# The first microseconds of a fused attention and gMLP block: order and split of the first loads, and who makes the first hT

## The chip, the cores and the metric

One core of one Trainium2 chip. The metric is the device time of one execution in microseconds (us), the median of several runs. The profile's span is 1.7 to 1.9 us shorter than the device time of the same execution. "Tile 1" is the second 128 rows of x, and "scores" are the matmuls of Q with K.

## The reference, cut to what matters

```python
mod = (_silu(c) @ w_mod).reshape(c.shape[0], 6, 1, -1)     # c: (1, 512), w_mod: (512, 3072)
sa, ca, ga, sb, cb, gb = (mod[:, i] for i in range(6))
h = _layernorm(x, axis=-1) * (1 + ca) + sa                 # x: (1, 2048, 512)
x = x + ga * _A_ref(h, A_k_cache, A_v_cache, A_wq, A_wo)   # q = h @ wq, 32 heads; 8 K and V heads; softmax; @ wo
h = _layernorm(x, axis=-1) * (1 + cb) + sb
x = x + gb * _B_ref(h, B_w_in, B_w_sp, B_b_sp, B_w_out)    # gMLP
```

All tensors are bf16. Before the first score can be computed the kernel needs: the modulation columns sa and ca (the first 1024 columns of w_mod), x tile 0 normalised, transposed and modulated (hT), the query weights of the first group, and K transposed.

## The kernel before

The prologue is one hand-ordered list of instructions. `warm(n)` issues n matmuls of zeros that nothing reads. `bank("misc")` and `bank("o_ps")` are tiles of one bank in PSUM, the memory into which TensorE (PE in the profiles) writes, `bank2()` one of two banks (s_ps); each name has two buffers. Line numbers in profiles of before: L868 is `mod_part`, L900 the transposes of xn, L883 those of K, L921 the first query product, L929 its two copies, L980 the scores, L846 the tile-1 transposes.

```python
nc.scalar.dma_start(out=c_bf[:], in_=c_dram)
nc.sync.dma_start(out=x_sb[:, 0, :], in_=x_dram[:, 0, :])
for kt in range(NDT):                                       # four row parts, 256 KB each
    nc.sync.dma_start(out=wmod_a[:, kt, :], in_=wmod_dram[:, kt, 0 : 2 * D])
load_k_nat(0)                                               # K, first 512 rows
load_wq(0, nc.sync)                                         # query weights, 512 KB
load_k_nat(1)
nc.sync.dma_start(out=x_sb[:, 1:CT, :], in_=x_dram[:, 1:CT, :])      # x tiles 1 to 3
# ... (K rows 1024 and up by DMA transpose, V, more x)
xns0 = ln1_norm(0, 1, ln1_stats(0, 1))
warm(10)
for kt in range(NDT - 1):
    mod_part(kt, mc_ps)                                     # 8 one-column matmuls
    warm(2)
x_ps = []
for half in range(2):                                       # dt 0, 1 in misc; dt 2, 3 in o_ps
    x_ps.append(bank(("misc", "o_ps")[half])[:].bitcast(BF16))
    # ... two transposes of xn each
mod_part(NDT - 1, mc_ps)
mod_copy(0, mc_ps)
for k in range(2):
    ln1_mod(hTs[0][:, k, 0:P], x_ps[0][:, k * P : (k + 1) * P], k)          # DVE: dt 0, 1
    nc.scalar.activation(out=hTs[0][:, 2 + k, 0:P], in_=x_ps[1][...], ...)  # ACT: dt 2, 3
k_turn((0, 1, 2, 3), (nc.vector.tensor_copy, nc.scalar.copy))               # K, through o_ps
q_ps = bank2()
for n, dt in enumerate((0, 2, 1, 3)):
    # ... four query matmuls, one for each head
for hf, copy in enumerate((nc.vector.tensor_copy, nc.scalar.copy)):
    copy(out=qTs[0][:, 2 * hf : 2 * hf + 2, 0:P], in_=...)  # both halves out of q_ps
warm(1)
# ... units of 8 slots; slot i: score pair i, exp; in unit 0 also tile 1 to 3 of hT and Q
```

## Time and profile before

| | device time, us | note |
|---|---|---|
| first runs | 1323.93 median of 3 | 1323.85 to 1324.84 |
| the profiled run | 1325.52 | span 1323.7; slower than each of the three |
| first rounds with the changed kernel | 1324.12 median of 6 | 1323.85 to 1325.55; the three first runs are among them |
| later rounds | 1324.24, 1324.15, 1324.05 medians of 9 | 1323.75 to 1324.95 |

The prediction below shows the lines on which it rests: the busy time of PE and the chain of waits of the first 16 us.

### The profile page before, as it was taken

What the parts mean: (1) busy time and instruction counts of PE and PEld (TensorE: products, weight loads), DVE (VectorE), ACT (ScalarE), POOL (GpSimd) and SP (SyncE); (2) the same over time, 40 slices, a digit from 0 to 9 for tenths busy, and PEclk for the clock granted to TensorE, in tenths of its full rate; (3) what the DMA queues carried; (4) which work ended last, traced back from release to release, by engine and by line L of the source; (5) the groups of instructions that cost most, each with busy time, mean ns of one, the idle gap of its engine ahead of it and who ended that gap; (6) DMA issues with size and microseconds to landing.
All of it is one profiled execution on the core that took longest, in us unless ns stands there. A gap on an engine that the chain in (4) does not pass through costs nothing.

```text
span 1323.7 us, 27668 instructions
## 1 busy us (share of the span) xinstructions
PE 1303.0 (98%) x12127; PEld 859.5 (65%) x12332; DVE 472.6 (36%) x1166; ACT 1077.6 (81%) x1061; POOL 48.9 (4%) x92
## 2 busy tenths in 40 slices
PE   8999999999999999999999999999999999999998
PEld 5666666666666666666666666666666666644445
DVE  5632222222222222222222222222222566794444
ACT  6898999999999999999999999999999999650000
POOL 1200000000000000000000000000000000020000
PEclk9999999999999999999999999999999999999999
DMA  7451022102111112111110221121101111143300
GB/s 175 114 135 30 17 49 37 36 15 53 21 33 33 33 37 37 29 37 37 33 33 17 53 37 29 21 53 17 33 17 21 25 30 33 33 114 80 70 21 26
DMA packets 148208, 58.12 MB, mean 44 GB/s; under 512 B 138384, under 2 KB 143760, under 8 KB 148080
## 3 DMA queue, kind: packets, MB, share of 16 engines
q1 hardware_dynamic: 141424, 37.78, 15.0%
q0 software_dynamic: 4208, 16.39, 4.1%
q10 hardware_dynamic: 2448, 2.10, 0.5%
q8 instruction: 98, 1.61, 0.5%
q14 instruction: 30, 0.25, 0.1%
HBM read 21.37 MB, written 2.10 MB: 18 GB/s over the span
## 4 chain that ended last, share of the span: by engine, by line
PE 98%; issue 1%; DMA 0%; DVE 0%; SPq 0%; ACT 0%; ACTq 0%
PE s_ps L980 36%; PE o_ps L1002 35%; PE misc L947 7%; PE misc L1347 7%; PE misc L1034 6%; PE s_ps L1193 2%; PE s_ps L1232 2%; PE o_ps L1368 1%; PE s_ps L1368 0%; DMA wmod_a<-in_w_mod_dram 0%; PE misc L1104 0%; PE s_ps L921 0%; DVE tmp L1380 0%; DVE yout L1381 0%; PE misc L1355 0%
## 5 line engine op out<-in xcount | busy, mean ns | idle before, releaser
L987 ACT ACTIVATE pT<-s_ps 128x1024 bf16<-128x1024 f32 x1024 | 1044.3, 1025 | 83.2 <-PE s_ps L980 9.2
L1002 PEld LDWEIGHTS <-pT 128*128 128x128 bf16 x8192 | 548.5, 98 | 241.2
L1002 PE MATMUL o_ps<-v,pT 128*128 128x129 bf16 x8192 | 631.4, 220 | 0.0
L980 PE MATMUL s_ps<-qT,kT 128*128 128x512 bf16 x2048 | 609.2, 379 | 10.2 <-ACT qT L929 0.5
L1013 DVE RECIPROCAL rall<-o_ps 128x2 f32<-128x2 f32 x256 | 43.7, 171 | 744.7 <-PE o_ps L1002 744.5
L980 PEld LDWEIGHTS <-kT 128*128 128x128 bf16 x2048 | 199.4, 98 | 119.2 <-issue 1.4
L947 PE MATMUL misc<-hT,wq_g 128*128 128x512 bf16 (+2 forms) x466 | 166.6, 370 | 0.1
L1034 PE MATMUL misc<-wo_g,oT 128*128 128x512 bf16 x386 | 146.3, 379 | 0.0
L1014 DVE TENSOR_TENSOR onorm<-o_ps,rall 128x256 bf16<-128x256 f32 x256 | 108.6, 424 | 9.0 <-DVE rall L1013 0.3
L1347 PE MATMUL misc<-wsp,z 128*128 128x512 bf16 (+2 forms) x555 | 100.5, 336 | 0.6 <-issue 0.3
L958 DVE CAST qT<-misc 128x512 bf16<-128x512 f32 x127 | 86.3, 680 | 2.4 <-PE misc L947 2.3
L1347 PEld LDWEIGHTS <-z 128*128 128x128 bf16 x560 | 50.6, 98 | 48.5
L1047 DVE TENSOR_TENSOR xacc<-misc,xacc 128x512 f32<-128x512 f32 x112 | 76.1, 679 | 0.0
L947 PEld LDWEIGHTS <-wq_g 128*128 128x128 bf16 x528 | 50.6, 98 | 1.1 <-issue 0.2
L1034 PEld LDWEIGHTS <-oT 128*128 128x128 bf16 x512 | 50.1, 98 | 0.8
L1362 DVE TENSOR_TENSOR gb<-misc,bsp_bc 128x512 bf16<-128x512 f32 (+1 forms) x28 | 18.4, 658 | 59.2 <-PE misc L1347 59.2
L1193 PE MATMUL s_ps<-win_sb,hT 128*128 128x448 bf16 x128 | 27.0, 352 | 0.1
L1203 ACT ACTIVATE z<-s_ps 128x896 bf16<-128x896 f32 x16 | 14.7, 917 | 14.9 <-PE s_ps L1193 14.9
L1232 PE MATMUL s_ps<-hT,win_sb 128*128 128x512 bf16 x109 | 24.3, 379 | 0.2
L1240 ACT ACTIVATE z1T<-s_ps 128x1024 bf16<-128x1024 f32 x14 | 14.3, 1024 | 10.1 <-PE s_ps L1232 9.1
L691 DVE BATCH_NORM_STATS2 bnst<-x_sb 128x6 f32<-128x512 bf16 x32 | 21.9, 683 | 0.5
L715 POOL DMA_DIRECT2D wq_g<-in_A_wq_dram x7 | 5.3, 752 | 420.9 <-PE misc L947 420.9
(86 smaller groups left out, 283.0 us busy)
## 6 DMA issues: line engine op xcount, KB each, us to landing
wq_g<-in_A_wq_dram POOLq DMA_DIRECT2D x7, 512.0 KB, 3.9
v<-in_A_v_cache_dram POOLq DMA_DIRECT2D x7, 512.0 KB, 6.9
wo_g<-in_A_wo_dram POOLq DMA_DIRECT2D x7, 512.0 KB, 4.7
oT<-onorm SPq DMA_TRANSPOSE x128, 2.4
wsp<-in_w_mod_dram POOLq DMA_DIRECT2D x1, 2048.0 KB, 10.3
out_dram<-yout ACTq DMA_DIRECT2D x16, 128.0 KB, 1.7
win_sb<-in_B_w_in_dram POOLq DMA_DIRECT2D x1, 1792.0 KB, 7.9
x_sb<-in_A_x_dram SPq DMA_DIRECT2D x3, 512.0 KB, 5.6
```

Of the source, the lines that this page charges most:

```text
L947: nc.tensor.matmul(ps[0][:, o0 : o0 + n], lhsT=wqs[g][:, dt, hh * DH : (hh + 1) * DH], rhs=hTs[ch][:, dt, c0 : c0 + n], start=(dt == 0), s ...
L958: nc.vector.tensor_copy(out=dst, in_=src)
L980: nc.tensor.matmul(s_ps[:, h * 512 : (h + 1) * 512].rearrange("p (r q) -> p r q", r=REP), lhsT=groups[g]["kT"][:, kt * P : (kt + 1) * P], ...
L987: nc.scalar.activation(out=pTs[u][:, 2 * i : 2 * i + 2, :], in_=s_ps[:].rearrange("p (k q) -> p k q", k=2), func=ACT.Exp, scale=inv_sqrt_dh,)
L1002: nc.tensor.matmul(o_ps[:, hh % 2, 0 : DH + 1], lhsT=pTs[u][:, kt, hh * P : (hh + 1) * P], rhs=groups[g]["v1"][:, kt, 0 : DH + 1], start=( ...
L1013: nc.vector.reciprocal(out=rall[:, c0 : c0 + 2], in_=o_ps[:, :, DH])
L1014: nc.vector.tensor_tensor(out=onorms[u][:, hh - 1 : hh + 1, :], in0=o_ps[:, :, 0:DH], in1=rall[:, c0 : c0 + 2].unsqueeze(2).to_broadcast([ ...
L1034: nc.tensor.matmul(X_ps[:], lhsT=oTs[u][:, hh, :], rhs=groups[g]["wo"][:, hh, :], start=(hh == 0), stop=(hh == REP - 1),)
L1047: nc.vector.tensor_tensor(out=xaccs[j][:], in0=X_ps[:], in1=xaccs[j][:], op=ALU.add)
L1193: nc.tensor.matmul(ps[0][:, hf * 512 : hf * 512 + FC], lhsT=h2Ts[j // CT][:, dt, (j % CT) * P : (j % CT + 1) * P], rhs=win_sb[:, dt, FH + ...
L1232: nc.tensor.matmul(ps[0][:, k * 512 : (k + 1) * 512], lhsT=win_sb[:, dt, f * P : (f + 1) * P], rhs=h2Ts[2 * ch2 + k][:, dt, :], start=(dt ...
L1347: nc.tensor.matmul(g_ps[:, :n], lhsT=z2[:, st, f * P : (f + 1) * P], rhs=wsp[t][:, st, c0 : c0 + n], start=(st == 0), stop=(st == NT - 1 a ...
```

## The change

Its intent: have the modulation columns, the query weights and K land in the order in which the first scores need them, and let the first query matmuls start as soon as one quarter of hT is there.

```diff
-    nc.sync.dma_start(out=x_sb[:, 0, :], in_=x_dram[:, 0, :])
-    for kt in range(NDT):
-        nc.sync.dma_start(out=wmod_a[:, kt, :], in_=wmod_dram[:, kt, 0 : 2 * D])
+    nc.scalar.dma_start(out=x_sb[:, 0, :], in_=x_dram[:, 0, :])
+    for i in range(2):
+        part = slice(i * D, (i + 1) * D)
+        nc.sync.dma_start(out=wmod_a[:, :, part], in_=wmod_dram[:, :, part])
-    load_k_nat(0)
-    load_wq(0, nc.sync)
+    wqs[0] = early.tile([P, NDT, REP * DH], BF16, name="wq_g")
+    for dts in (slice(0, 2), slice(2, 4)):
+        nc.sync.dma_start(out=wqs[0][:, dts, :], in_=wq_dram[:, dts, 0 : REP * DH])
+    load_k_nat(0)
     load_k_nat(1)
# ... mod_part sums a column part, all kt of a column in a row; mod_columns goes (cut)
     warm(10)
-    for kt in range(NDT - 1):
-        mod_part(kt, mc_ps)
-        warm(2)
+    mod_part(0, wmod_a, 0, mc_ps)
+    warm(6)
+    x_ps = [bank("misc")[:].bitcast(BF16), bank2()[:, 0:512].bitcast(BF16)]   # dt % 2 picks one
# ... four transposes of xn
-    mod_part(NDT - 1, mc_ps)
+    mod_part(1, wmod_a, D, mc_ps)
     mod_copy(0, mc_ps)
+    warm(2)
# hT: DVE makes dt 0 and 2, ACT 1 and 3 (before: DVE 0 and 1, ACT 2 and 3)
-    k_turn((0, 1, 2, 3), (nc.vector.tensor_copy, nc.scalar.copy))
-    q_ps = bank2()
-    for n, dt in enumerate((0, 2, 1, 3)):
+    q_ps = [bank("misc"), bank2()]
+    for dt in range(NDT):
+        if dt == 2:
+            k_turn((0, 1, 2, 3), (nc.vector.tensor_copy, nc.scalar.copy))
# ... the query matmuls and the two copies, from q_ps[0] and q_ps[1]
-    warm(1)
+    warm(2)
```

Line numbers in profiles of the changed kernel: L848 modulation, L807 and L899 hT on DVE and ACT, L912 first query product, L870 K transposes, L920 copies of Q, L971 scores, L825 tile-1 transposes, L779 warm-ups.

More of the change, by code (lines that the diff above doesn't have):

```diff
@@ L782, in warm @@
             )
-    def mod_columns(first, wmod, i0):
-        mc_ps = bank("misc")
-        for i in range(2):
-            for dt in range(NDT):
-                col = i * NDT + dt
-                w0 = (first + i - i0) * D + dt * P
-                for kt in range(NDT):
-                    nc.tensor.matmul(
-                        mc_ps[:, col : col + 1],
-                        lhsT=wmod[:, kt, w0 : w0 + P],
-                        rhs=sc_bf[:, kt : kt + 1],
-                        start=(kt == 0),
-                        stop=(kt == NDT - 1),
-                    )
-        mod_copy(first, mc_ps)
-    def mod_copy(first, mc_ps):
-        c0 = first * NDT
-        nc.vector.tensor_copy(out=modc[:, c0 : c0 + NDT], in_=mc_ps[:, 0:NDT])
-        nc.vector.tensor_scalar_add(
-            out=modc[:, c0 + NDT : c0 + 2 * NDT], in0=mc_ps[:, NDT : 2 * NDT], scalar1=1.0
-        )
     def ln1_stats(j0, n):
@@ L863, in ln1_dma_mod, with mod_part, mod_copy @@
             ln1_mod(hTs[ch][:, dt, :], hTs[ch][:, dt, :], dt)
-    def mod_part(kt, mc_ps):
-        for col in range(2 * NDT):
-            nc.tensor.matmul(
-                mc_ps[:, col : col + 1],
-                lhsT=wmod_a[:, kt, col * P : (col + 1) * P],
-                rhs=sc_bf[:, kt : kt + 1],
-                start=(kt == 0 and col == 0),
-                stop=(kt == NDT - 1 and col == 2 * NDT - 1),
-            )
+    def mod_part(i, wmod, w0, mc_ps):
+        for dt in range(NDT):
+            for kt in range(NDT):
+                nc.tensor.matmul(
+                    mc_ps[:, i * NDT + dt : i * NDT + dt + 1],
+                    lhsT=wmod[:, kt, w0 + dt * P : w0 + (dt + 1) * P],
+                    rhs=sc_bf[:, kt : kt + 1],
+                    start=(kt == 0),
+                    stop=(kt == NDT - 1),
+                )
+    def mod_copy(first, mc_ps):
+        c0 = first * NDT
+        nc.vector.tensor_copy(out=modc[:, c0 : c0 + NDT], in_=mc_ps[:, 0:NDT])
+        nc.vector.tensor_scalar_add(
+            out=modc[:, c0 + NDT : c0 + 2 * NDT], in0=mc_ps[:, NDT : 2 * NDT], scalar1=1.0
+        )
     def k_turn(kts, copies):
@@ L891 @@
     warm(10)
-    for kt in range(NDT - 1):
-        mod_part(kt, mc_ps)
-        warm(2)
-    x_ps = []
-    for half in range(2):
-        x_ps.append(bank(("misc", "o_ps")[half])[:].bitcast(BF16))
-        for k in range(2):
-            dt = 2 * half + k
-            nc.tensor.transpose(
-                x_ps[half][:, k * P : (k + 1) * P], xns0[0][:, dt * P : (dt + 1) * P], ident[:]
-            )
-    mod_part(NDT - 1, mc_ps)
+    mod_part(0, wmod_a, 0, mc_ps)
+    warm(6)
+    x_ps = [bank("misc")[:].bitcast(BF16), bank2()[:, 0:512].bitcast(BF16)]
@@ L904 @@
+    for dt in range(NDT):
+        nc.tensor.transpose(
+            x_ps[dt % 2][:, dt // 2 * P : (dt // 2 + 1) * P],
+            xns0[0][:, dt * P : (dt + 1) * P],
+            ident[:],
+        )
+    mod_part(1, wmod_a, D, mc_ps)
     mod_copy(0, mc_ps)
+    warm(2)
     hT_of(0)
     for k in range(2):
-        ln1_mod(hTs[0][:, k, 0:P], x_ps[0][:, k * P : (k + 1) * P], k)
-        nc.scalar.activation(
-            out=hTs[0][:, 2 + k, 0:P],
-            in_=x_ps[1][:, k * P : (k + 1) * P],
-            func=ACT.Identity,
-            scale=modc[:, NDT + 2 + k : NDT + 3 + k],
-            bias=modc[:, 2 + k : 3 + k],
-        )
@@ L915 @@
-    k_turn((0, 1, 2, 3), (nc.vector.tensor_copy, nc.scalar.copy))
+        for dt in (2 * k, 2 * k + 1):
+            dst, src = hTs[0][:, dt, 0:P], x_ps[dt % 2][:, k * P : (k + 1) * P]
+            if dt % 2 == 0:
+                ln1_mod(dst, src, dt)
+            else:
+                nc.scalar.activation(
+                    out=dst,
+                    in_=src,
+                    func=ACT.Identity,
+                    scale=modc[:, NDT + dt : NDT + dt + 1],
+                    bias=modc[:, dt : dt + 1],
+                )
@@ L916 @@
     qTs = {0: early.tile([P, REP, 512], BF16, name="qT")}
-    q_ps = bank2()
-    for n, dt in enumerate((0, 2, 1, 3)):
+    q_ps = [bank("misc"), bank2()]
+    for dt in range(NDT):
+        if dt == 2:
+            k_turn((0, 1, 2, 3), (nc.vector.tensor_copy, nc.scalar.copy))
         for hh in range(REP):
-            c0 = hh // 2 * 512 + hh % 2 * P
             nc.tensor.matmul(
-                q_ps[:, c0 : c0 + P],
+                q_ps[hh // 2][:, hh % 2 * P : (hh % 2 + 1) * P],
                 lhsT=wqs[0][:, dt, hh * DH : (hh + 1) * DH],
@@ L924 @@
                 rhs=hTs[0][:, dt, 0:P],
-                start=(n == 0 and hh % 2 == 0),
-                stop=(n == NDT - 1 and hh % 2 == 1),
+                start=(dt == 0 and hh % 2 == 0),
+                stop=(dt == NDT - 1 and hh % 2 == 1),
             )
@@ L930 @@
             out=qTs[0][:, 2 * hf : 2 * hf + 2, 0:P],
-            in_=q_ps[:, hf * 512 : hf * 512 + 2 * P].rearrange("p (h q) -> p h q", h=2),
+            in_=q_ps[hf][:, 0 : 2 * P].rearrange("p (h q) -> p h q", h=2),
         )
-    warm(1)
+    warm(2)
     def qproj(b, heads, c0, n):
@@ L1099, in mod_lhs, with mod_cols_b @@
         return lhs
+    def mod_cols_b():
+        mc_ps = bank("misc")
+        for i in range(2):
+            mod_part(i, wmod_b, (1 + i) * D, mc_ps)
+        mod_copy(3, mc_ps)
     def mod_row(row_out, i, lhs):
@@ L1155 @@
     at(8, 1, lambda: rest_w.update(lhs=mod_lhs()))
-    at(9, 4, lambda: mod_columns(3, wmod_b, 2))
+    at(9, 4, mod_cols_b)
     at(10, 4, lambda: mod_row(ga_rows, 2, rest_w["lhs"]))
```

## The prediction

> **What bounds the kernel now.** I read the page first, part 1 and part 4. TensorE is busy for 1303.0 of 1323.7 us and the chain that ended last is 98% PE. The parts of it that weigh are the score, value and projection matmuls of the steady state, none of which the change touches.
>
> ```profile
> PE 1303.0 (98%) x12127; PEld 859.5 (65%) x12332; DVE 472.6 (36%) x1166; ACT 1077.6 (81%) x1061; POOL 48.9 (4%) x92
> ...
> PE 98%; issue 1%; DMA 0%; DVE 0%; SPq 0%; ACT 0%; ACTq 0%
> ```
>
> The reader is to see how little is left: 1323.7 - 1303.0 = 20.7 us without a matmul, everywhere in the kernel. The edit is all in the prologue, before the first score matmul (L980), so I read the chain of waits in order of time next, for the first 24 us. Columns: start, duration, what.
>
> ```profile
> 2.14 5.42 DMA wmod_a<-in_w_mod_dram
> 7.60 0.35 PE misc L868 x8
> ...
> 8.85 0.16 DVE modc L803
> 9.01 0.08 DVE modc L804
> 9.18 0.82 ACT hT L908 x2
> 10.04 0.34 PE o_ps L883 x2
> 10.37 1.72 PE s_ps L921 x16
> 12.12 0.44 DVE qT L929
> 12.58 0.38 ACT qT L929
> 13.00 0.83 PE s_ps L980 x2
> 13.83 0.24 PE o_ps L883 x4
> 14.09 0.42 DVE kT L886
> ...
> 15.69 0.40 PE misc L846 x4
> ```
>
> This is one serial string. The modulation weight lands, its columns are summed (L868), copied (L803, L804), applied to hT by ACT (L908); two K transposes wait for ACT because they use the o_ps bank that ACT was reading; then 16 query matmuls; then DVE and, only after it, ACT copy qT; at 13.00 the scores start. From about 24 us on, the same view has PE pieces end to end. So a microsecond taken off this string comes off the end, and nothing bigger than this string can be won. The stretches view (busy time per engine, then granted clock, DMA share, GB/s) shows one more thing:
>
> ```profile
> 9.50:10.00 0.50, 0.00 (x0) 0.00 (x0) 0.41 (x2) 0.48 (x2) 0.00 (x0) 1.00 1.79 309
> 10.00:10.50 0.50, 0.47 (x6) 0.46 (x6) 0.00 (x0) 0.09 (x1) 0.00 (x0) 0.60 2.22 168
> 10.50:11.00 0.50, 0.50 (x7) 0.50 (x6) 0.00 (x0) 0.28 (x1) 0.00 (x0) 0.50 0.49 35
> ...
> 13.50:14.00 0.50, 0.50 (x7) 0.35 (x6) 0.00 (x0) 0.13 (x1) 0.42 (x2) 0.98 1.40 223
> ```
>
> After the PE gap of 9.0 to 10.0 us the clock is halved, until about 13.5 us, so the query matmuls and the first score pair run at half speed: 16 in 1.72 us is 108 ns each, where 13 query matmuls of the same shape later take 0.89 us, 68 ns each; a score pair takes 0.83 us here and 0.43 us later.
>
> **What the Trainium skill says.** "TensorE: Matmul & The Clock Gate", section "What's actually happening": the array runs at half clock unless a free-running window of 3413 ns was busy. The trace agrees: the half-clock stretch is about 3.4 us (10.1 to 13.5). As the window is not tied to the kernel's start, where it falls may differ between executions. "DMA: Bandwidth & Descriptors", section "Queues, rings and completion order": each DMA engine takes the descriptors of one ring in order, and SP's and ACT's loads are separate rings on the same engines. The trace agrees in the order of landings (below). Same page, "Why small descriptors are slow": a fixed cost per packet; the 2 KB rows of the modulation weight become 1 KB rows here, and I count it as a small loss; no view so far measures it. "PSUM — Partial Sum Buffer", section "PSUM bank collisions raise a hardware error": two engines must be kept off one bank at the same time. The trace shows the price: 1.07 us in which L883 waits for ACT hT L908.
>
> **The change, part by part.**
>
> *Loads.* From the tile views, issue start plus issue-to-landing: the four modulation quarters are issued at 1.21 to 2.6 and take 2.8 to 5.6 us, so they land at about 4.0, 6.0 (a weight load waits for it until 6.06), 7.56 (2.14 + 5.42) and 8.2. K's first half lands at 3.08 + 5.5 = 8.6, the query weights at 3.57 + 6.5 = 10.07, x tiles 1 to 3 at 4.59 + 6.9 = 11.5. The ring is served in order, so I take a landing time to belong to a place in the line, that is, to the bytes ahead of it. The new line is x tile 0 (on ACT's ring), modulation part 0 (512 KB), part 1, query half 0, half 1, K half 0, K half 1, x 1 to 3. Part 1 stands where the last quarter stood: **8.2**. Part 0 stands where the second quarter stood: 6.0. K half 0 now ends where the query weights ended: **10.07**, 1.5 us later than before. Query half 1 is 128 KB ahead of that, about 9.7, and half 0 about 9.0 (at some 300 GB/s, from the stretches). x 1 to 3 keeps 11.5. Smaller packets may cost 0.1 to 0.3 us, an earlier first issue (0.73 for 1.21) gives some back; I keep 0.15 us of loss.
>
> *Modulation columns.* The same 32 one-column matmuls, 16 + 16 instead of 4 times 8. After the last landing 16 run, not 8. Eight take 0.35 us with their fill, and their weight loads come 0.04 us apart, so 8 more are about 0.2 to 0.3 us. The 8 of before also stood behind two warm-up matmuls and the transposes, which now stand before the wait. I call that even: modc is ready at 9.1 as before.
>
> *hT and the first query matmuls.* DVE does dt 0 and 2, ACT 1 and 3, from separate banks, and the query matmuls go in the order 0, 1, then 2, 3. DVE's two took 0.59 us, so dt 0 is there at 9.11 + 0.3 = 9.4 and dt 1 from ACT at 9.18 + 0.45 = 9.6. Eight query matmuls thus fit at 9.45 to 10.0, in what is now the PE gap. Then four K transposes, which wait for K at 10.07 instead of for ACT at 9.99: the ready time hardly moves, but eight matmuls already lie behind it. At 10.1 + 0.24 (four transposes, L883 at 13.83) = 10.35 only 8 query matmuls are left instead of 16. Saved: 8 x 108 ns = **0.86 us**.
>
> *Clock.* If the shorter gap, and the warm-ups (6 before the transposes, 2 after the columns), keep the clock full, the other 8 take 8 x 68 instead of 8 x 108 ns: **0.32 us**; and the first score pair 0.43 instead of 0.83: **0.40 us**. If a half-clock window falls there anyway, these are not had. I give 60% to keeping it.
>
> *qT copies.* Two PSUM tiles instead of one. Before, ACT started at 12.58, when DVE's was over at 12.54. Now both start together: **0.38 + 0.06 = 0.44 us** saved. The two warm-ups behind lie under this copy.
>
> *Sum.* To the start of the scores 0.86 + 0.44 = 1.30 us for sure, 0.32 + 0.40 more with the clock: 0.6 x 0.72 = 0.43. Less 0.15 for packets: 1.6 us. First score at about 11.5 instead of 13.00. The next part of the string is DVE: qT copy, statistics of x tile 1, kT copy, statistics of tile 2, xn, then the transposes at 15.69. Tile 1 is only there at 11.5, so: 11.5 + 0.69 + 0.18 = 12.4, kT copy to 12.85, statistics and aggregate to 13.7, xn to 14.1, transposes at about 14.1. That allows 15.69 - 14.1 = 1.6 us, no more. I take **1.45 us** as what arrives at the steady state. Afterwards nothing changes but the place of a helper for the second modulation columns: same matmuls, same slot.
>
> **Rivals.**
> 1. *K becomes the wait.* It was loaded early and now comes last of the three. If it lands at 11 instead of 10.07, the string is held by K and the gain falls to 0.5 us or so, for a time near 1323.5. For it: K is moved behind 512 KB. Against: the query weights of before, at the same place in the line, landed at 10.07.
> 2. *The modulation weight lands no earlier, or later.* Half-size packets and a first part that needs 512 KB before anything can run. If part 1 lands at 9 instead of 8.2, 0.8 us of the gain goes, near 1323.2. Against: by bytes its place in the line is the same.
> 3. *Clock lottery.* A half-clock window that falls on the score matmuls of 11 to 15 us costs up to 1.7 us (half of 3.4). Then the gain is zero: 1324. The other way, no half-clock window at all: 2 us won, 1321.9.
> 4. *A hidden gain.* ACT sets the pace of the first 8 exponentials (1.03 us each), so a faster start could be lost in waits for ACT. Against: ACT was idle 0.9, 0.75 and 0.35 us between them, waiting for PE; they move with the start.
>
> **Range and chances.** 1323.93 - 1.45 = 1322.5 us. The three runs of before spread over 1.0 us, the rivals take away up to 1.5, the full clock adds 0.5: 1321.0 to 1324.0 holds it 8 times in 10. Two per cent is 26 us, more than the whole prologue before the steady state; only a broken schedule later could reach it. Faster by over 2%: 0.003; within 2%: 0.99; slower: 0.007.
>
> **What would show it.** In the profile of the changed kernel: the first L971 score matmul near 11.5 us, not 13.0; the modulation part 1 landing near 8.2 and K half 0 near 10.1; the query matmuls in two groups of 8, around four K transposes that wait for a DMA; the two qT copies starting together; a granted clock of 1.00 in most of 10 to 13.5 us; the steady state from then on unchanged in each group's mean. The prediction would be wrong if a load lands a microsecond late, if the clock drops in another window that costs as much, or if the start moves and a later wait (x tile 1, the exponentials) gives it back.

## The result, and the profile after

| | before, median us | changed, median us | ratio, 95% |
|---|---|---|---|
| first rounds (6 and 6 runs) | 1324.12 | 1322.84 | 0.9989 (0.9976 to 1.0002) |
| again, other rounds (9 and 5) | 1324.15 | 1323.38 | 0.9993 (0.9979 to 1.0006) |

A ratio is the mean time of one kernel's runs over that of the other's in the same rounds, so it is not quite the ratio of the medians. Both intervals include 1: by times alone a gain of 0.8 to 1.3 us is at the edge of what such rounds can show. The runs do keep apart: the eleven of the changed kernel took 1322.65 to 1323.50 us, and no run of before, in any round, took less than 1323.55. All outputs are right. The traces show what changed.

The changed kernel's chain of waits in order of time (start, duration, what):

```profile
4.35 6.38 DMA x_sb<-in_A_x_dram
...
10.75 0.70 DVE bnst L691
...
12.79 0.32 DVE xn L680
...
13.15 0.40 PE misc L825 x4
13.55 0.43 PE s_ps L971 x2
```

Set it against the chain of before in the prediction: the tile-1 transposes start at 13.15, where before they started at 15.69 us. In this execution the chain begins with the landing of x tiles 1 to 3 at 10.73 us and not with the scores, but the two strings end almost together: tile 1 starts 2.52 us after the scores here, and 2.45 or 2.46 us after them in e2, e3, e7 and e9, where the chain goes through the scores. So a still earlier score would gain almost nothing here, and the earlier landing of these tiles (10.73 instead of 11.46 us) is needed for the gain. Now the instructions in order of time (start, duration, engine, line, what, count; in brackets the idle time of the engine before it, and what ended it):

```profile
8.79 0.27 PE L912 MATMUL misc<-hT,wq_g 128*128 128x128 bf16 x2 [0.34 <-DVE hT L807]
...
9.33 0.40 PE L870 MATMUL o_ps<-ident,kT 128*128 128x128 bf16 x4
...
10.10 0.42 DVE L920 CAST qT<-misc 128x256 bf16<-128x256 f32 x1 [0.15 <-PE misc L912]
10.21 0.37 ACT L920 CAST qT<-s_ps 128x256 bf16<-128x256 f32 x1
...
10.63 0.59 PE L971 MATMUL s_ps<-qT,kT 128*128 128x512 bf16 x2
```

The first query matmuls wait for DVE's first quarter of hT, and then PE hardly waits: eight, the K transposes, eight more, and both copies of Q at once. K came just in time: it landed at 9.3 us, and its transposes start 0.21 us after the pair of query matmuls ahead of them, in e9 0.11 us. The scores start at 10.63 instead of 13.00 us. The stretches view of the changed kernel (stretch, its length, busy time of PE, PEld (weight loads), DVE, ACT, POOL, granted clock as a share of full speed, DMA share, GB/s) has no half-clock stretch:

```profile
9.50:10.00 0.50, 0.50 (x12) 0.50 (x10) 0.29 (x1) 0.24 (x1) 0.00 (x0) 1.00 2.35 211
10.00:10.50 0.50, 0.50 (x6) 0.11 (x2) 0.40 (x1) 0.43 (x2) 0.00 (x0) 1.00 0.42 29
10.50:11.00 0.50, 0.47 (x3) 0.25 (x3) 0.27 (x2) 0.08 (x1) 0.00 (x0) 1.00 1.15 255
12.50:13.00 0.50, 0.00 (x0) 0.00 (x0) 0.47 (x3) 0.50 (x1) 0.14 (x1) 1.00 1.42 219
```

The last line shows what is left: PE idles while DVE works, until the xn of tile 1 is there. Part 1 of the page, the line of busy times:

```profile
PE 1312.4 (99%) x12335; PEld 858.3 (65%) x12335; DVE 473.5 (36%) x1166; ACT 1077.8 (82%) x1061; POOL 49.4 (4%) x92
```

PE seems 9 us busier than before. It is not: before's page counts 12127 matmuls against 12332 weight loads, so about 200 matmul records are missing from that trace. The changed kernel's counts agree. Such a pair of counts is to be compared before busy times are. The prediction's 20.7 us without a matmul is too much for the same reason; the changed kernel's page leaves 1321.5 - 1312.4 = 9.1 us.

What comes back later? Nothing, in either direction. In all profiles in which the order of unit 0 is as before, the span is the start of the tile-1 transposes plus 1307.95 to 1308.35 us: 1323.7 - 15.69 = 1308.0 before, 1321.5 - 13.15 = 1308.35 after, 1323.4 - 15.14 = 1308.3 in the slowest experiment. So the start of these transposes, read from one profile, measures a version to 0.2 us where the times scatter by 0.5. But it is that one execution's value.

The puzzle: this pair of profiles is 2.2 us apart in span, the medians 1.28 and 0.77 us.

### The profile page after: what moved, and what is told of

The parts are those of the page before. It is cut to its first block, busy times and chain, and to the rows that moved or that the text cites. A ratio compares the mean times of both kernels' runs of the same rounds, so it can differ in the third digit from the quotient of the medians.

```text
span 1321.5 us, 27879 instructions
## 1 busy us (share of the span) xinstructions
PE 1312.4 (99%) x12335; PEld 858.3 (65%) x12335; DVE 473.5 (36%) x1166; ACT 1077.8 (82%) x1061; POOL 49.4 (4%) x92
## 4 chain that ended last, share of the span: by engine, by line
PE 98%; DMA 0%; DVE 0%; SPq 0%; issue 0%
PE o_ps L993 35%; PE s_ps L971 33%; PE misc L1025 8%; PE misc L938 8%; PE misc L1344 7%; PE s_ps L1190 2%; PE s_ps L1229 2%; PE o_ps L1365 1%; PE s_ps L1365 1%; DMA x_sb<-in_A_x_dram 0%; PE misc L1101 0%; DVE tmp L1377 0%; DVE yout L1378 0%; DVE bnst L691 0%; SPq L700 0%; SPq L745 0%
## 5 line engine op out<-in xcount | busy, mean ns | idle before, releaser
L971 PE MATMUL s_ps<-qT,kT 128*128 128x512 bf16 x2048 | 609.0, 379 | 0.0
L971 PEld LDWEIGHTS <-kT 128*128 128x128 bf16 x2048 | 199.3, 98 | 118.7 <-DVE qT L920 0.5
L1025 PE MATMUL misc<-wo_g,oT 128*128 128x512 bf16 x512 | 194.0, 379 | 0.0
L938 PE MATMUL misc<-hT,wq_g 128*128 128x512 bf16 (+2 forms) x528 | 189.6, 371 | 0.0
L1200 ACT ACTIVATE z<-s_ps 128x896 bf16<-128x896 f32 x16 | 14.7, 917 | 14.9 <-PE s_ps L1190 14.9
```

The lines of the kernel that those rows point to most:

```text
L938: nc.tensor.matmul(ps[0][:, o0 : o0 + n], lhsT=wqs[g][:, dt, hh * DH : (hh + 1) * DH], rhs=hTs[ch][:, dt, c0 : c0 + n], start=(dt == 0), s ...
L971: nc.tensor.matmul(s_ps[:, h * 512 : (h + 1) * 512].rearrange("p (r q) -> p r q", r=REP), lhsT=groups[g]["kT"][:, kt * P : (kt + 1) * P], ...
L1025: nc.tensor.matmul(X_ps[:], lhsT=oTs[u][:, hh, :], rhs=groups[g]["wo"][:, hh, :], start=(hh == 0), stop=(hh == REP - 1),)
```

## The experiments

Two theories. **The string** (the path theory): the gain is a shorter chain of landings, hT, query matmuls, copies. **The clock**: the gain is that a half-clock stretch of 3.4 us no longer falls into the prologue. A third possibility was that a part is hidden, behind the landing of x tiles 1 to 3. The table has all runs; times are means of five runs, "before" the mean of nine runs of before in the same rounds, then the start of scores and of tile-1 transposes in the one profile, and when the trace first records the full clock (below: when the array wakes).

| run | mean us | before | difference | scores | tile 1 | full clock from |
|---|---|---|---|---|---|---|
| the kernel before (profile of the prediction) | | | | 13.00 | 15.69 | 6.7; half 10.1 to 13.5 |
| the changed kernel (6 runs each) | 1322.89 | 1324.40 | -1.5 | 10.63 | 13.15 | 3.8 |
| e0_before_again | 1324.08 | 1324.33 | -0.3 | 11.62 | 14.70 | 4.4; half 11.3 to 14.7 |
| e1_rows | 1323.22 | 1324.33 | -1.1 | 10.73 | 13.21 | 6.2 |
| e2_k_early | 1323.29 | 1324.33 | -1.0 | 10.66 | 13.11 | 5.0 |
| e3_hT_as_before | 1323.48 | 1324.33 | -0.8 | 11.43 | 13.88 | 7.2 |
| e9_after_again | 1323.26 | 1324.17 | -0.9 | 11.07 | 13.53 | 7.1 |
| e5_few_warm | 1324.52 | 1324.17 | +0.3 | 12.06 | 15.14 | 13.6 |
| e6_before_gap_warm | 1324.27 | 1324.17 | +0.1 | 12.00 | 15.05 | 5.2; half 12.1 to 15.5 |
| e7_loads_alone | 1324.04 | 1324.17 | -0.1 | 11.55 | 14.00 | 6.5 |
| e4_one_qps | 1323.56 | 1324.10 | -0.5 | 10.95 | 13.40 | 4.6 |
| e10_old_loads | 1323.95 | 1324.10 | -0.2 | 12.18 | 14.63 | 5.6 |
| e11_no_added_warm | 1323.25 | 1324.10 | -0.9 | 11.16 | 13.62 | 7.1 |
| e8_scores_first | 1322.66 | 1324.10 | -1.4 | 10.46 | | 5.0 |

The same kernel can differ by 0.25 us from itself (e0), so differences below 0.3 us mean nothing in these times. The -1.5 of the first rounds leans on one run of before of 1325.55 us; without it, it is -1.3.

### e0_before_again: is the profile of before typical?

The kernel before, not edited.

> The kernel before, unchanged. In the two traces the first score matmul moved from 13.00 to 10.63 us (2.4 us) and the span from 1323.7 to 1321.5 us (2.2), but the medians of the timed runs differ by only 1.28 us. Clock theory: the profiled execution of before had its half-clock window (10.1 to 13.5 us) in an unlucky place, and most executions have it elsewhere. Then this profile shows the window at another time or not at all, and a span nearer 1322.5; the granted clock of the runs takes two values, 0.998 and 0.999. Path theory: the window is caused by the idle PE of 9.0 to 10.0 us, so it is in nearly every execution, the first score is again at about 13.0, all clocks are 0.998, and 2.2 us is what the change gives in every pair of executions. Ratio 1.000.

Measured: 1324.15 us median. The second profile's chain of waits:

```profile
3.56 6.03 DMA wq_g<-in_A_wq_dram
...
9.64 1.08 PE s_ps L921 x16
...
11.62 1.01 PE s_ps L980 x2
...
14.70 0.40 PE misc L846 x4
```

The query matmuls took 1.08 us here, 67 ns each and not 108, and the half-clock stretch sits over the first scores. What the 16 matmuls wait for is another thing too: not ACT and the K transposes but **the landing of the query weights**, at 9.59 us. Tile 1 starts a whole microsecond earlier than in the first profile. So the first profile was an unlucky execution, and the typical string of before is shorter. The mean time of before less the 1.8 us between device time and span, less 1308.15, gives an estimate of 14.1 to 14.5 us for its typical tile-1 start; the same sum for the changed kernel (1322.9 to 1323.3) gives 12.9 to 13.3. That is the measured gain, 0.9 to 1.5 us.

Neither theory's forecast came out whole: the half-clock stretch is there again, but at another time. What it is worth can be read from the runs. Of the 32 runs of before in the later rounds (e0's five among them), six have a granted clock of 0.997 or 0.998 and took 1324.73 us in the mean; the 25 with 0.999 took 1324.04. So a low clock goes with some 0.7 us, which in six runs of 32 makes about 0.1 us of before's mean (an estimate).

The record also has runs that can hold no such stretch: 3.4 us at half clock lose 1.7 of some 1322 us, or 0.0013 of the clock, and a clock of 1.000 leaves room for less than half of that. With 1.000, before took 1324.41 us and e6 (before with four more warm-ups) 1324.01 and 1324.07; the changed kernel took 1322.87. So about 1 us of gain is there without a half-clock stretch on either side. These are few runs, and what lies ahead of a trace's first clock record does not count in this figure.

### e1_rows: the modulation weight in row parts

```diff
-    for i in range(2):
-        part = slice(i * D, (i + 1) * D)
-        nc.sync.dma_start(out=wmod_a[:, :, part], in_=wmod_dram[:, :, part])
+    for kt in range(NDT):
+        nc.sync.dma_start(out=wmod_a[:, kt, :], in_=wmod_dram[:, kt, 0 : 2 * D])
```

(with the sum by row part, and the six warm-ups in pairs between)

> The changed kernel with the modulation weight again in four row parts (2 KB rows) and its columns summed by row part; all else as changed, x tile 0 still on ACT's ring. Before, the last quarter landed at about 8.2 us; after, the last part lands at 1.48 + 5.9 = 7.4 us. Theory A (shape): the 2 KB rows with 24 KB between them are slow to fetch (0.105 to 0.141 us a packet at 2 to 5 us where 0.084 is the floor, against 0.047 for 1 KB). Then the last part lands at about 8.0 again, first score at about 11.2 and half of the gain is lost: ratio about 0.9994. Theory B (start): it landed early because the first issue came at 0.73 instead of 1.21 us. Then it lands at about 7.4 to 7.6, first score 10.6 to 10.8, ratio 0.999.

The last part landed at 7.5 us, as theory B had it; tile 1 at 13.21 and -1.1 us: as good as the changed kernel. Theory A falls. The split of the modulation weight into two column parts is not where the gain is.

### e2_k_early: K ahead of the query weights

```diff
-    wqs[0] = early.tile([P, NDT, REP * DH], BF16, name="wq_g")
-    for dts in (slice(0, 2), slice(2, 4)):
-        nc.sync.dma_start(out=wqs[0][:, dts, :], in_=wq_dram[:, dts, 0 : REP * DH])
     load_k_nat(0)
+    load_wq(0, nc.sync)
     load_k_nat(1)
```

> The changed kernel with the first half of K ahead of the query weights, and these in one load, as before. The line of bytes is the same, so the query weights land last, at about 9.2 us (where K half 0 landed in the changed kernel, by 9.3), instead of 8.7 for their first half. If the order matters by the first query matmuls (path theory): they start at 9.3 instead of 8.79, all 16 lie behind the landing, first score about 11.1, 0.4 to 0.5 us later, and the time 0.3 us above the changed kernel's. If x tile 1, which lands at 10.7 us in both, sets what follows, the score starts later but the transposes of tile 1 stay at 13.15 us and the time does not move.

The query weights, in one load behind K, landed at 8.86 us and the first query matmul started at 8.91, 0.1 us later than in the changed kernel. Scores at 10.66, tile 1 at 13.11, -1.0 us. So this order, with one load instead of two halves, costs nothing that shows, and I had this landing too late (9.2 us).

### e3_hT_as_before

```diff
-    x_ps = [bank("misc")[:].bitcast(BF16), bank2()[:, 0:512].bitcast(BF16)]
+    x_ps = []                       # dt 0, 1 in misc; dt 2, 3 in o_ps, as before
...
-    for dt in range(NDT):
-        if dt == 2:
-            k_turn((0, 1, 2, 3), (nc.vector.tensor_copy, nc.scalar.copy))
+    k_turn((0, 1, 2, 3), (nc.vector.tensor_copy, nc.scalar.copy))
+    for n, dt in enumerate((0, 2, 1, 3)):
```

> The changed kernel with hT split as before (DVE 0 and 1, ACT 2 and 3 through an o_ps bank, K transposes ahead of all query matmuls). Path theory: the last K transposes wait for ACT's second hT at 9.2 us, the 16 query matmuls run at 9.4 to 10.4 at full clock, first score at about 11.0 instead of 10.63; about 0.3 to 0.4 us of the gain is from this part. Clock theory: the PE gap comes back (8.0 or 8.5 to 9.2), the window is halved again, 16 matmuls take 1.7 us and the first score is at 12; about 1 us of the gain is lost. Rival: hidden behind x tile 1 at 10.7 us, no difference in time.

The first score came at 11.43 us, not at 11.0 as the path theory had it, but the array also woke later than in the profile that it was reckoned from. The fair comparison is with e9, whose array woke at the same time (7.1 and 7.2 us) and whose modulation ended within 0.03 us: tile 1 at 13.88 against 13.53, so this part is worth 0.35 us in the string, as the string theory said. In the times it is lost in the noise (1323.48 against 1323.26 in other rounds). The clock stayed full.

### e9_after_again

The changed kernel, not edited.

> The changed kernel, unchanged, for a second profile and for a comparison in the same rounds as the parts. Path theory: first score at 10.6 us within 0.3, transposes of tile 1 at 13.1 to 13.4, 1.2 to 1.5 us below the kernel before (ratio 0.9989 to 0.9991), whatever the phase of the clock. Clock theory: where a half-clock window falls into 7 to 14 us, the gain is gone in that run and the five times spread by over 1 us.

1323.38 us median, 0.9 us below before by means, less than the 1.2 to 1.5 that the path theory forecast; scores at 11.07 and tile 1 at 13.53 us are also a little later than forecast. Its chain of waits is not that of the first profile:

```profile
5.63 0.41 PE misc L848 x16
6.04 1.91 PE o_ps L779 x6
7.94 0.06 PE misc L884
...
8.16 0.39 PE misc L848 x16
```

Six warm-ups took 2.05 us in its timeline (1.91 of them are on this chain), against 1.46 us in the changed kernel's first profile, because the array became fast only at 7.1 us. They end after the second modulation part has landed (1.48 + 5.8 = 7.3 us), so here the warm-ups themselves are on the string. In the changed profiles with the full clock from 3.8 to 6.2 us tile 1 starts at 13.1 to 13.4 (e4's 13.4 and e3's 13.9 include their own edits); with 7.1 to 7.2 at 13.5 to 13.9. The moment at which the array wakes accounts for about 0.4 us of the scatter.

### e5_few_warm, e11_no_added_warm: which warm-ups matter

```diff
     mod_part(0, wmod_a, 0, mc_ps)
-    warm(6)                         # e5 only
...
     mod_copy(0, mc_ps)
-    warm(2)                         # e5 and e11
...
-    warm(2)
+    warm(1)                         # e5 and e11
```

> The changed kernel without the 6 warm-ups after the first modulation part and the 2 after the second, and with 1 instead of 2 before the scores. Clock theory: the array falls to half clock at some point of 7 to 14 us in most executions; the 16 query matmuls take 1.7 instead of 0.9 us, a score pair 0.83 instead of 0.43; first score at 11.4 or later, ratio 0.9995 or above. Path theory: the warm-ups are off the string (they lie in waits for a landing or for hT), so a half-clock window costs at most 0.4 us and the time stays within 0.3 us of the changed kernel's.

> The changed kernel without the warm-ups that the change added (2 behind the second modulation part, 1 of 2 ahead of the scores), but with the 6 that were there before as three pairs. Without all of them the gain was lost whole (1324.5, the array at half clock until 13.6 us). If the added ones are what keeps the clock: a half-clock window in 7 to 14 us in the profile, 16 query matmuls at 108 ns, time 1324 or above in some runs. If the 6 old ones are what wakes the array: full clock, tile-1 transposes at 13.1 to 13.6, time 1323.2 to 1323.5.

e5 lost the whole gain (+0.3 us against before). Its chain:

```profile
9.31 0.37 PE misc L910 x2
9.68 0.21 PE s_ps L910 x2
...
10.32 0.43 PE o_ps L870 x4
...
12.06 1.01 PE s_ps L969 x2
...
15.14 0.40 PE misc L825 x4
```

Two query matmuls in 0.21 us are 105 ns each, half speed, and a score pair takes 1.01 us. The path theory's "off the string" was wrong: the warm-ups earn their place by the state they leave the array in. In e5 PE was busy for only 0.5 of each of 7 to 8 and 8 to 9 us, and the full clock first came at 13.6 us. But e11 (1323.25 us mean, tile 1 at 13.62) is as good as the changed kernel: the six that before also had, as three pairs, are enough; the three that the change added do nothing that these runs show.

### e6_before_gap_warm: fill before's gap

```diff
     mod_copy(0, mc_ps)
+    g_ps = bank2()
+    for _ in range(4):
+        nc.tensor.matmul(g_ps[:, 0:512]..., lhsT=zeros[:, 0, :], rhs=zeros[:], start=True, stop=True)
```

> The kernel before plus four warm-up matmuls into a spare score bank, in the idle second of PE between the last modulation column and the K transposes that wait for ACT (they take 0.9 us of 1.07 us of idle time). Clock theory: the half-clock window of 10.1 to 13.5 us (11.3 to 14.7 in the second profile) goes, 16 query matmuls take 0.9 to 1.1 us, scores about 0.4 to 0.8 us earlier, and the time falls by 0.5 us or more: ratio 0.9996 or below. Path theory: most of before's time is not in the window (a timed execution of before with a granted clock of 1.000 took 1324.41 us, no faster than the others), so the time stays within 0.3 us of before.

No gain (1324.27 against 1324.17). The 16 query matmuls ran at full clock, 1.08 us from 10.02, but they waited for the query weights until 9.97 us, and a half-clock stretch came all the same, later, at 12.1 to 15.5 us. In before, one wait hides behind another: the query weights' landing holds the same matmuls as the K transposes' wait. e6 leaves that wait in place and fills it; e10, below, takes it away.

### e7_loads_alone and e10_old_loads: either half without the other

e7 has the new loads and before's order of work; e10 the new work and before's loads:

```diff
 # e10, against the changed kernel
-    nc.scalar.dma_start(out=x_sb[:, 0, :], in_=x_dram[:, 0, :])
+    nc.sync.dma_start(out=x_sb[:, 0, :], in_=x_dram[:, 0, :])
+    # wmod_a in four row parts, load_k_nat(0), load_wq(0, nc.sync), load_k_nat(1)
```

> The loads of the changed kernel alone (x tile 0 on ACT's ring, the modulation weight in two column parts with 6 warm-ups between, query weights in halves ahead of K), with hT, K transposes, query order, one PSUM tile for the query and the last warm-up as before. Path theory: the modulation lands 0.8 us earlier, but K half 0 only at 9.3 us; K transposes then, 16 query matmuls, two copies in a row: first score at about 11.6 to 12.0, which is 1.2 of 2.4 us and as early as before's second profile (11.62). Time 0.5 us below before. If the loads are everything, it is as fast as the changed kernel; if the order of loads needs the new order of work, no faster than before.

> The changed kernel's work (hT alternating, two PSUM tiles, all warm-ups) with all loads as before: x tile 0 first on SP's ring, the modulation weight in four row parts, K half 0 ahead of one load of the query weights. Loads alone gave nothing (1324.04 mean against 1324.17), and undone singly the two splits cost nothing. If the gain is in the work and the loads are idle decoration: tile-1 transposes at 13.1 to 13.6, 0.9 us or more below before. If the two belong together (the query weights land at 9.6 to 10.1 us in three profiles of before's loads, so all 16 query matmuls wait for them): scores at 11.2 to 11.6, tile-1 transposes at 13.8 to 14.1, and at most half of the gain is left, ratio 0.9996 to 1.000.

e7 gives 1324.04 and e10 1323.95 us, 0.1 and 0.2 below before: **neither half gives a gain that these rounds can show; together they give 0.9 or more.** A few tenths of a microsecond in either half cannot be excluded. The path theory had forecast 0.5 us for e7, and for e10 scores at 11.2 to 11.6 us: both were missed, on the side of less gain. The chains say why. e7's:

```profile
3.31 5.84 DMA kT<-in_A_k_cache_dram
...
9.20 0.54 PE o_ps L870 x4
9.74 0.91 PE s_ps L907 x16
...
10.67 0.44 DVE qT L915
...
11.13 0.38 ACT qT L915
...
11.55 0.59 PE s_ps L966 x2
```

K landed at 9.15 us. With K last and all work behind K, 16 query matmuls and two copies in a row follow the landing. e10's:

```profile
3.56 6.82 DMA wq_g<-in_A_wq_dram
...
10.43 0.29 PE misc L920 x2
...
12.18 0.59 PE s_ps L979 x2
```

With before's loads the query weights land at 10.38 us (9.6 to 10.4 in the four profiles of these loads), and a quarter of hT that is there at 8.6 us has nothing to multiply. e10 has a full clock throughout, in spite of 2 us without a matmul, and is no faster for it.

What made the query weights land earlier in the new loads? e1 undid the column parts, e2 the order and the halves, and they landed by 9.0 us in both. With x tile 0 on ACT's ring they are issued at 2.8 us (e2) and 3.1 us (e1, the second half) and take 5.6 to 6.1 us; with all of before's loads they are issued at 3.56 us and take 6.0 to 6.8. So part is the earlier issue; which of the loads ahead makes the rest was not tested singly and stays open.

### e4_one_qps

```diff
-    q_ps = [bank("misc"), bank2()]
+    q_ps = bank2()                  # halves in its two banks, as before
```

> The changed kernel with one two-bank PSUM tile for the first query product, as before. In eight profiles the span was the start of the tile-1 transposes plus 1308.0 to 1308.35 us, so each part is judged by that start. Path theory: ACT's qT copy begins only when DVE's is over, scores start 0.4 us later (about 11.1 to 11.4 us), and of this 0.1 to 0.4 us reaches the tile-1 transposes (13.3 to 13.9), as kT copy and statistics of tile 2 follow the K transposes behind the scores. Rival: the string of x tile 1 (lands at 10.7, statistics, rstd on GpSimd, xn) hides it, tile-1 transposes at 13.1 to 13.5 as in the changed kernel and no loss of time. Time 1323.3 to 1323.7 against 1323.3.

ACT's copy started when DVE's was over (10.53 us), scores at 10.95, tile 1 at 13.40: 0.25 us behind the first profile of the changed kernel, which woke and summed the modulation at nearly the same times. In time 1323.56 against 1323.25 (e11, same rounds), 0.3 us. The string theory holds, at about two thirds of the 0.44 us predicted.

e4's trace also shows a cost of the change that the prediction did not have. On ACT's ring x tile 0 landed at 4.7 us, where before it landed at 3.0, so its xn is ready at 7.1 us instead of 6.3. In e4 the chain goes through it: the transposes of xn start at 7.15, and the second modulation part, which landed at 7.3 us, is summed behind them at 7.55. No run put x tile 0 alone back on SP's ring.

### e8_scores_first: a version meant to beat both

```diff
-    at(0, 2, first_turn)
-    at(0, 5, lambda: ln1_turn(2, 2, first["x2"]))
+    fill[0, 2].append(first_turn)               # behind score pair 2, not ahead of it
-    fill[0, 3] = qproj(0, list(range(REP)), P, P)
+    fill[0, 4] += qproj(0, list(range(REP)), P, P)
+    fill[0, 5] = [lambda: ln1_turn(2, 2, first["x2"])]
-    fill[0, 6], fill[0, 7], fill[1, 0] = rest_q[0:5], rest_q[5:11], rest_q[11:16]
+    fill[0, 7], fill[1, 0] = rest_q[0:11], rest_q[11:16]
```

> A version meant to beat the changed kernel: in the first unit the score pairs of slots 2 and 4 go ahead of the tile-1 transposes and the tile-1 query product, slot 5's ahead of the tile-2 and 3 transposes, and slot 7's ahead of the next query product. PE idles 1.0 us (12.1 to 13.1) for the xn of tile 1 in every profile of the changed kernel; a score pair takes 0.43 us and its data are there. So 0.4 to 0.6 us less: time 1322.7 to 1322.9, ratio 0.9987 to 0.999. If ACT's exponentials (1.03 us each) or the DVE string of tile 1 to 3 set the end of that stage, no gain: 1323.3.

1322.65 us median (1322.31 to 1323.10), 1.4 below before and, by means, 0.6 below e11 in the same rounds, whose runs (1323.07 to 1323.58) hardly overlap and which elsewhere equals the changed kernel. The changed kernel itself was not in these rounds, and in its best rounds it was 1.5 below before, so that e8 beats it rests on e11 and on the traces. Its chain:

```profile
10.46 0.61 PE s_ps L971 x2
...
11.09 2.86 ACT pT L978 x3
...
14.00 0.59 PE s_ps L971 x2
```

Three exponentials now run end to end, 2.86 us, and set the pace; the PE gap of 12.1 to 13.1 us is partly filled with a score pair. The first product with V starts at 19.30 us, 0.76 and 1.13 us before that of the two profiles of the changed kernel (20.06, 20.43); its span is 1320.6 against 1321.5 and 1321.7 us.

## Why the prediction was right or wrong

The time, 1322.84 us, lies in the range, 0.3 us from the point; the second rounds' 1323.38 too. The working was less right than the sum.

- **Where it counts: right.** All that happens is ahead of the tile-1 transposes, and it arrives at the end undiminished (1307.95 to 1308.35 us behind them in every profile). The rival "a hidden gain" is out.
- **Baseline: the first error.** The step "one serial string" was read from a single execution, which took 1325.52 us where only one other run of before took over 1325. Typical executions of before start tile 1 at an estimated 14.1 to 14.5, not 15.69 us. "8 x 108 ns = 0.86 us" was mis-sized: at the typical speed eight matmuls are 8 x 67 = 0.54 us, and e3 shows 0.35 us for this part. The clock term of 0.43 us stands for the 0.72 us of that one execution; the clocks of the runs give about 0.1 us in the mean (an estimate, see e0).
- **Landings: the second error, the other way.** "A landing time belongs to a place in the line, that is, to the bytes ahead of it" failed. Modulation part 1 landed at 7.4 and not 8.2, K half 0 at 9.15 (e7) and not 10.07, x tiles 1 to 3 at 10.73 and not 11.5 us. Part of this is the untypical execution again: with the same loads the last modulation quarter landed at 7.2, 7.2 and 6.7 us in e0, e6 and e10, so the changed kernel does not have the modulation earlier than usual. What it has earlier are the query weights, whole at 8.7 to 9.0 us instead of 9.6 to 10.4, and x tiles 1 to 3 (before's loads: 11.0 to 11.8 us). The rest is the step itself: K half 0 has as many bytes ahead of it as the query weights of before, which landed at 9.6 or later in all four profiles. Scores came at 10.63 and 11.07 instead of 11.5, tile 1 at 13.15 and 13.53 instead of 14.1. The two errors nearly cancel in the difference: that the point is within 0.3 us is partly luck.
- **A wait left out.** The working has the query weights landing at 10.07 us and the query matmuls starting at 10.1 to 10.4 us in before, and still gave the whole wait to ACT and the K transposes. e6 and e10 show the second wait: the work alone gains nothing with the old loads. The prediction let the 0.86 and 0.44 us stand as "for sure"; they need the new loads.
- **qT copies: right in kind,** 0.44 predicted, 0.25 to 0.3 measured by e4.
- **Packets: no loss.** 0.15 us was put in for smaller rows; with the large rows (e1) the last part landed at 7.5 us, with the small ones at 7.4.
- **Rivals.** K landed at 9.3 us and held its transposes for about 0.1 us only; the modulation came at its usual time (7.0 to 7.6 us, with before's loads 6.7 to 8.2); the clock does play its lottery, worth some 0.7 us in about one run of before in five, and without the six warm-ups (e5) it takes the whole gain.

## What to carry to other kernels

A profile is one execution: before a string of a few microseconds is taken apart, compare its run with the timed runs, and profile it twice. The profiled execution is the first of each list of runs, and in seven of the 13 lists it was the slowest. Where two waits end within some tenths of a microsecond of each other, taking one away gains little; list what else each instruction needed and when that was there. And judge changes of a microsecond by the start of the first instruction behind which all is constant, since it resolves what the times can't.

## What the Trainium skill lacked or had wrong

- "TensorE: Matmul & The Clock Gate", section "Why this matters for your kernels", asks for no idle gaps above about 3 us. Here half-clock stretches of 3.41 us followed windows with much less: in the first profile of before one gap of 1.07 us, and 1.3 us idle in the whole 3.41 us ahead; 1.7 us idle in e0 and e6. But in e10 the same stretch of 3.41 us from 9.0 us on, counted on from its first clock record, had 1.5 us without a matmul, and the clock stayed full. Where the line lies is not settled here.
- No page that I read warns that a view built on a trace's clock record shows full clock ahead of the first record. The stretches view of before shows 1.00 from the start, where ten 512-column warm-ups took 4.45 us, 445 ns each, against 216 ns later; in e5 it shows 1.00 where query matmuls ran at half speed.
- "DMA: Bandwidth & Descriptors", section "Issuing engines are not separate DMA queues", calls the issue time saved by a second engine usually small relative to the DMA itself. For one load that holds here: an issue on SP took 0.41 to 0.93 us, a load 2.3 to 6.9 us to land. But the issues of one engine add up: x tiles 1 to 3, ninth in before's line on SP, were issued at 4.59 us, and with x tile 0 on ACT the first modulation load was issued at 0.73 instead of 1.21 us. The same page's warning about small packets did not bite at this size: 1 KB rows of the modulation weight were no slower than 2 KB rows (last part landed at 7.4 and 7.5 us).
